# A joined attention and mixture-of-experts kernel: routing groups of 6, 6, 4, 4, 2 and 2 tiles, a narrower running state, and the weight splits of the attention loop partly moved to its ending

## The chip, the core and the metric

The kernel runs on one core of a Trainium2 chip. The metric is the device time of one execution in microseconds (us); the median of three runs is given. Engines are named as in the profile: PE (TensorE) multiplies matrices, PEld is its weight loading, DVE is VectorE, ACT is ScalarE, POOL is GpSimd, SP is the engine whose queue starts most transfers.

## The reference

Three layers, one after the other, all in float32:

```
state = alpha[t] * state + k[t] (outer) v[t];  y[t] = q[t] @ state      # 4 batches x 8 heads, 768 steps, head size 48
x = y as [3072 tokens, 384]
idx = argmax(normalised x @ normalised emb.T / tau); gate = softmax(...)[idx]
x2 = gate * (relu(x @ w1[idx]) @ w2[idx])                                # 8 experts, 384 -> 1024 -> 384
out = elu(x2 @ w_in) @ w_out                                            # 384 -> 2048 -> 384
```

## The kernel before, in words

**Tiles.** The 768 steps are cut into 6 chunks of 128, the work into 24 tiles (chunk times batch); tile i belongs to batch i mod 4. Within a tile the recurrence is done as matrix products: the decays are accumulated by two scans on DVE, R (backwards, line 311) and A (forwards, line 321); POOL makes the scaled keys Kh (line 314) and queries Qh (line 323) from them; PE forms the scores psS (line 351), DVE masks them into P (line 358, two halves), PE multiplies P with the values (line 374) and the queries with the running state G (line 371) into psY, and makes the tile's contribution psU to the state (line 382). DVE adds psU to G (line 394), and ACT scales G by the chunk's decay (line 406). There are four states G, one a batch, each with its own 128-wide slices per pair of heads of which 112 columns are used; the two off-diagonal blocks of a pair are computed and are zero or unused by construction of the value tile `vt`, 176 wide per pair (`VW`).

**Rows and routing.** PE turns psY into token rows and logits in one product (psX, line 419, step `stD`); ACT copies the rows out to `xt`, takes their squares, and DVE reduces the logits `lg` (line 424). When a group of tiles (`GROUPS`: 8, 8, 4, 2 and 2 tiles) is done, DVE finds each token's expert (`stR1`), PE counts places (`stR2`), DVE makes the row numbers `pos_i`, then come the gates (`stX`, `gates`). Each tile's rows are then scaled on ACT (`scale_x`) and scattered to the experts' regions in DRAM by an indirect transfer from POOL (`put`, line 529, after a small memset `tick`).

**The loop.** All of this is written out by hand in program order. In turn i (i = 0 to 21 of `fast`) SP loads tile i+3, PE does the scores of tile i+1, DVE the scans of tile i+2 and P of tile i+1, PE the output of tile i. Every engine works through its own list in this order. `todo` holds the small routing operations on DVE, of which a turn does at most 12. In turn i > 9 one piece of the first expert's weights is split into a rounded part `whi` (ACT, line 175) and a rest `wlo` (DVE, line 178): 12 pieces in all, each rest done in the turn after its `whi` (list `lag`), and each rest starting the load of another piece (`load_w`). `ending` does the last two tiles, the last routing groups, and the first expert's rows: those of the last two tiles come by a product with a one-hot matrix (`hot`, `first_x`, line 541), the rest by a load of the scattered rows (`xr`, line 249) which waits for all earlier scatters, and they meet in the same accumulators (line 893).

**After the loop.** Eight experts, then the dense layer: PE is busy there nearly all the time. None of that is edited.

Of the kernel before, what the change touches and what calls it, by code (L numbers as in the profile page):

```python
# [25 lines left out]
C2 = 112  # L26
TP = T + 1
SW = H // 2 * TP + 1
VW = 176
# [5 lines left out]
GROUPS = [list(range(8)), list(range(8, 16)), list(range(16, 20)), [20, 21], [22, 23]]  # L35
NMID = 9
AHEAD = 4
NG = len(GROUPS)
# [21 lines left out]
def fused_kernel(ctx, tc, qk, a, v, emb, w12, wi, wo, cst, sel, cols, out):  # L60
# [91 lines left out]

    def load_w(n=1):

        for _ in range(n):
            if nload[0] < len(pieces):
                e, s, j = pieces[nload[0]]
                t = stage.tile([128, PW], F32, tag="raw", name="raw")
                nc.sync.dma_start(out=t, in_=w12[e, :, s * SLOT + j * PW:s * SLOT + (j + 1) * PW])
                raw[nload[0]] = t  # L160
                nload[0] += 1

    def split_piece(lag=None):

        if npc[0] >= len(pieces):
            return
        n = npc[0]
        e, s, j = pieces[n]
        npc[0] += 1
        if j == 0:  # L170
            whi[e, s] = ring.tile([128, SLOT], F32R, tag="whi", name="whi")
            wlo[e, s] = ring.tile([128, SLOT], F32R, tag="wlo", name="wlo")
        sl = slice(j * PW, (j + 1) * PW)
        h, l, r = whi[e, s], wlo[e, s], raw.pop(n)
        nc.scalar.activation(out=h[:, sl], in_=r, func=AF.Copy)  # L175

        def low_part():
            nc.vector.tensor_tensor(l[:, sl], r, h[:, sl].bitcast(F32), op=ALU.subtract)  # L178
            load_w()

        if lag is None:
            low_part()
        else:
            lag.append(low_part)
# [76 lines left out]
    def attention():  # L261
        with ExitStack() as st:
# [5 lines left out]
            sm = st.enter_context(tc.tile_pool(name="sm", bufs=2))  # L268
            psD = st.enter_context(tc.tile_pool(name="psD", bufs=2, space=PS))
# [4 lines left out]
            G = [gp.tile([C2, NP, 128], F32, name=f"G{b}") for b in range(B)]  # L274
# [87 lines left out]
            def stC(i):  # L362
# [6 lines left out]
                if cc:  # L369
                    for p in range(NP):  # L370
                        nc.tensor.matmul(y[:, p], G[b][:, p], qh[:, p], start=(p == 0), stop=False)
                for p in range(NP):
                    for h2 in range(2):
                        nc.tensor.matmul(y[HP * h2:HP * (h2 + 1), p], vv[:, p, C2 * h2:C2 * h2 + HP], pp[:, h2, p], start=(cc == 0 and p == 0), stop=(p == NP - 1))
# [12 lines left out]
            def stG(i):  # L387

                if i not in U_:
                    return  # L390
                g3 = G[i % B][:, :, :C2]
                u3 = U_.pop(i)[:, :, :C2]
                if i >= B:
                    nc.vector.tensor_tensor(g3, u3, g3, op=ALU.add)
                else:
                    nc.vector.tensor_copy(g3, u3)

            def stH(i):

                if i >= NT:  # L400
                    return
                r = Rs.pop(i)
                if i >= B:
                    g = G[i % B]
                    for p in range(NP):
                        nc.scalar.activation(out=g[:, p, :C2], in_=g[:, p, :C2], func=AF.Copy, scale=seg(r)[:, p, 1:2])
# [140 lines left out]
            def general():  # L547
# [15 lines left out]
                with tc.For_i(0, NC, 1) as cc, tc.For_i(0, T // TB, 1) as tb:  # L563
                    ts = bass.ds(tb * TB, TB)
                    for b in range(B):
                        for p in range(NP):
                            for h2 in range(2):
                                p0 = (b * H + 2 * p + h2) * EG
                                ch = slice(h2 * HP, h2 * HP + D)
                                for nm, src in (("a", a[bass.ds(cc, 1), ch, b, bass.ds(tb * TB + (p * TP + 1), TB)]),  # L570
# [5 lines left out]
                                    in_=v[bass.ds(cc, 1), ts, b, p, C2 * h2:C2 * h2 + D].rearrange("o t (g e) -> (o g) t e", g=EG))  # L576
# [32 lines left out]
            def fast():  # L609
# [44 lines left out]
                for i in range(tail):  # L654
# [46 lines left out]
                    for j in putq[:2 if len(putq) > 5 else 1]:  # L701
# [6 lines left out]
                    if 9 <= i < 9 + AHEAD * PIECES:  # L708
                        split_piece(lag)
# [30 lines left out]
            def ending():  # L740
# [14 lines left out]
                x3 = stX(g2 - 1)  # L755
                run(x3 + gates(g2 - 1), late)
# [42 lines left out]
                pk[-1]()  # L799
                return xr, t0  # L800
# [366 lines left out]
def _layout(inputs):  # L1167
# [21 lines left out]
    for h2 in range(2):  # L1189
        vv[..., C2 * h2:C2 * h2 + D] = v6[..., h2, :]  # L1190
# [44 lines left out]
```

## Time and profile before

| | |
|---|---|
| median of 3 runs | 849.19 us (848.91 to 854.18) |
| profiled execution, time / span | 844.74 us / 843.0 us |
| PE, PEld, DVE, ACT, POOL busy in the span | 94%, 85%, 64%, 43%, 23% |
| granted clock of PE, mean | 0.984 of full speed |
| attention (loop and ending) | from 0 to about 182 us |
| experts and dense layer | about 182 to 843 us |

The busy shares of the whole span are those of the experts and the dense layer, which are four fifths of the time. The edits lie in the first fifth, so the profile has to be read by stage there: the busy times of a stretch, the engines' instructions in order of time, and what each waited for. A row of the timeline gives start, duration, engine, line, operation, output and inputs with their shapes, a count of merged instructions, and in brackets the idle time before it and what ended that. One float32 matmul of the program shows as two records.

### The profile page before, as it was taken

The numbers are of one execution on the slowest core, as the hardware profiler recorded it, in microseconds if no ns is written. First come the engines' busy times: TensorE is split into PE (matmuls) and PEld (weight loads), VectorE is DVE, ScalarE is ACT, GpSimd is POOL, SyncE is SP. The second block draws the span as 40 slices with busy tenths as digits, with TensorE's granted clock in tenths as the row PEclk, the third lists the DMA queues.
The fourth block names the chain that finished last, engine by engine and source line by source line (L and its number), as shares of the span: only waits on it lengthen the run. The fifth ranks groups of instructions, "written<-read, shape, count | busy, mean of one in ns | idle before, by whom it ended". The sixth has DMA issues, their size and how long they took to land.

```text
span 843.0 us, 13005 instructions
## 1 busy us (share of the span) xinstructions
PE 794.8 (94%) x4876; PEld 716.9 (85%) x4876; DVE 541.5 (64%) x997; ACT 361.6 (43%) x761; POOL 196.8 (23%) x218
## 2 busy tenths in 40 slices
PE   7797987789999999999999999999999999999996
PEld 5687876659988888999989889999999999999995
DVE  7787999846867757777556675545545545555442
ACT  2454775824544434554344543333333333333331
POOL 6333475722323324334200002002002002001102
PEclk9798999999999998999999999999999999999999
DMA  9599687545676774866200001001001000000001
GB/s 259 142 261 250 202 258 212 169 136 160 177 175 190 169 158 144 208 154 204 31 1 2 1 1 37 1 1 38 1 1 37 1 1 29 10 1 10 29 1 37
DMA packets 45234, 82.19 MB, mean 98 GB/s; under 512 B 11624, under 2 KB 18024, under 8 KB 45168
## 3 DMA queue, kind: packets, MB, share of 16 engines
q1 hardware_dynamic: 38512, 71.86, 32.0%
q0 software_dynamic: 3072, 9.45, 3.1%
q8 instruction: 39, 0.64, 0.3%
q10 hardware_dynamic: 3584, 0.01, 0.3%
q14 instruction: 27, 0.22, 0.1%
HBM read 69.10 MB, written 12.22 MB: 96 GB/s over the span
## 4 chain that ended last, share of the span: by engine, by line
PE 67%; DVE 4%; DMA 3%; ACT 2%; issue 1%; POOLq 0%; POOL 0%; SPq 0%; ACTq 0%; DVEq 0%
PE h L1092 21%; PE o L1115 7%; PE o L1113 7%; PE o L1114 7%; PE y L939 4%; PE y L940 4%; PE y L941 4%; PE h L910 4%; PE h L911 4%; PE h L909 4%; PE t L891 1%; DMA raw<-in_wo_dram 1%; DVE dlo L234 1%; DMA raw<-in_wi_dram 1%; DVE g L1098 1%; DVE mn L1094 1%
## 5 line engine op out<-in xcount | busy, mean ns | idle before, releaser
L1094 DVE TENSOR_SCALAR mn<-h 128x512 f32<-128x512 f32 x96 | 66.2, 689 | 139.1 <-PE h L1092 139.1
L1095 ACT ACTIVATE mn<-mn 128x512 f32<-128x512 f32 x96 | 60.7, 632 | 171.9 <-DVE mn L1094 171.9
L1115 PE MATMUL o<-dwo,gl 128*128 128x384 f32 x384 | 129.4, 337 | 1.4 <-DVE gl L1102 1.4
L1114 PE MATMUL o<-dlo,gh 128*128 128x384 f32 x384 | 128.4, 334 | 0.0
L1113 PE MATMUL o<-dwo,gh 128*128 128x384 f32 x384 | 128.2, 334 | 0.0
L1092 PE MATMUL h<-xh,dwi 128*128 128x512 f32 x288 | 112.7, 391 | 0.6 <-ACT x2T L953 0.6
L1092 PE MATMUL h<-xh,dlo 128*128 128x512 f32 x288 | 113.2, 393 | 0.0
L1092 PE MATMUL h<-xl,dwi 128*128 128x512 f32 x288 | 112.5, 392 | 0.0
L1124 POOL DMA_INDIRECT out_dram<-ob,ids x24 | 23.5, 981 | 369.7 <-DVE ob L1119 171.1
L1101 ACT ACTIVATE gh<-g 128x512 fp32r<-128x512 f32 x96 | 60.7, 633 | 77.6 <-DVE g L1098 77.6
L178 DVE TENSOR_TENSOR wlo<-raw,whi 128x512 fp32r<-128x512 f32 x96 | 77.6, 832 | 5.9 <-ACT whi L175 5.9
L913 ACT ACTIVATE hh<-h 128x432 fp32r<-128x432 f32 x64 | 33.9, 530 | 106.7 <-PE h L911 99.6
L1098 DVE SCALAR_TENSOR_TENSOR g<-mn,h 128x512 f32<-128x512 f32 x96 | 66.1, 688 | 16.0 <-ACT mn L1095 15.9
L1113 PEld LDWEIGHTS o<-dwo,gh 128*128 128x128 f32 x384 | 72.0, 187 | 4.2
L1114 PEld LDWEIGHTS o<-dlo,gh 128*128 128x128 f32 x384 | 72.0, 187 | 4.0
L939 PE MATMUL y<-hh,whi 128*128 128x432 f32 x192 | 71.9, 375 | 2.5 <-ACT hh L913 2.5
L1115 PEld LDWEIGHTS o<-dwo,gl 128*128 128x128 f32 x384 | 72.2, 188 | 2.1 <-DVE gl L1102 1.7
L914 DVE SCALAR_TENSOR_TENSOR hl<-h,hh 128x432 fp32r<-128x432 f32 x64 | 38.7, 604 | 54.8 <-ACT hh L913 53.5
L218 POOL TENSOR_SCALAR dg<-dg 128x384 f32<-128x384 f32 x32 | 41.4, 1292 | 131.1 <-ACT dg L217 131.1
L940 PE MATMUL y<-hl,whi 128*128 128x432 f32 x192 | 69.7, 363 | 2.1 <-DVE hl L914 2.1
L909 PE MATMUL h<-xh,whi 128*128 128x432 f32 x192 | 69.8, 364 | 0.7 <-ACTq L966 0.7
L911 PE MATMUL h<-xh,wlo 128*128 128x432 f32 x192 | 69.5, 362 | 0.0
(193 smaller groups left out, 1539.1 us busy)
## 6 DMA issues: line engine op xcount, KB each, us to landing
raw<-in_w_dram SPq DMA_DIRECT2D x96, 256.0 KB, 3.2
qk<-in_qk_dram SPq DMA_DIRECT2D x24, 448.0 KB, 6.2
vt<-in_v_dram SPq DMA_DIRECT2D x24, 352.0 KB, 6.9
raw<-in_wi_dram SPq DMA_DIRECT2D x16, 384.0 KB, 4.4
raw<-in_wo_dram SPq DMA_DIRECT2D x16, 384.0 KB, 4.5
at<-in_alpha_dram SPq DMA_DIRECT2D x24, 226.2 KB, 4.8
xr<-xs SPq DMA_DIRECT2D x7, 576.0 KB, 7.2
xs<-zero SPq DMA_DIRECT2D x7, 288.8 KB, 8.4
```

The lines of the kernel that those rows point to most:

```text
L178: nc.vector.tensor_tensor(l[:, sl], r, h[:, sl].bitcast(F32), op=ALU.subtract)
L909: nc.tensor.matmul(ps, wh, xh[:, kk], start=(kk == 0), stop=False)
L911: nc.tensor.matmul(ps, wl, xh[:, kk], start=False, stop=(kk == KD - 1))
L939: nc.tensor.matmul(acc[e][d], wh, hh, start=(f == 0), stop=False)
L940: nc.tensor.matmul(acc[e][d], wh, hl, start=False, stop=False)
L1092: nc.tensor.matmul(ps, l, x, start=(n == 0), stop=(n == len(terms) - 1))
L1094: nc.vector.tensor_scalar(mn, ps, 0.0, None, op0=ALU.min)
L1095: nc.scalar.activation(out=mn, in_=mn, func=AF.Exp)
L1098: nc.vector.scalar_tensor_tensor(g, mn, -1.0, ps, op0=ALU.add, op1=ALU.max)
L1113: nc.tensor.matmul(o_, gh[:, sl], wh, start=(f == 0), stop=False)
L1114: nc.tensor.matmul(o_, gh[:, sl], wl, start=False, stop=False)
L1115: nc.tensor.matmul(o_, gl[:, sl], wh, start=False, stop=(f == M - 1))
```

## The change

1. The value tile is 128 wide per pair of heads in place of 176 (`VW`), and the state's off-diagonal blocks are no longer computed: psU is 48 wide, G 64 wide, the product of queries and state is done per head (8 products of 48 rows and 64 columns in place of 4 of 112 rows and 128 columns).
2. The addition of psU to G moves from DVE to PE (a product of G with the identity opens psU's accumulation), and ACT copies the sum back into G, at the head of the next turn.
3. `GROUPS` is 6, 6, 4, 4, 2, 2.
4. The first four weight pieces are split as before; the rests (`wlo`) of the other eight are put off to `ending` (`split_spare`: two, one and five of them). Their raw pieces stay in a pool of their own (`early`, 8 buffers). `load_w` is called once a turn from turn 5 on, no longer from the rest.
5. In a turn `put` comes after `stA` and the second half of P, so that POOL does Qh ahead of the scatter; the second `put` of a turn and the second `scale_x` are allowed with one tile less waiting.
6. In `ending`, `stD` of tile 22 comes ahead of `stR2` of the fifth group.

```diff
-VW = 176
+VW = 128
-GROUPS = [list(range(8)), list(range(8, 16)), list(range(16, 20)), [20, 21], [22, 23]]
+GROUPS = [list(range(6)), list(range(6, 12)), list(range(12, 16)), list(range(16, 20)), [20, 21], [22, 23]]
+DIRECT = 4
+    def split_spare(n):
+        for _ in range(n):
+            if spare:
+                spare.pop(0)()
     def load_w(n=1):
...
-                t = stage.tile([128, PW], F32, tag="raw", name="raw")
+                pool = early_p[0] if DIRECT <= nload[0] < AHEAD * PIECES else stage
+                t = pool.tile([128, PW], F32, tag="raw", name="raw")
...
         def low_part():
             nc.vector.tensor_tensor(l[:, sl], r, h[:, sl].bitcast(F32), op=ALU.subtract)
-            load_w()
...
-            G = [gp.tile([C2, NP, 128], F32, name=f"G{b}") for b in range(B)]
+            G = [gp.tile([C2, NP, HP], F32, name=f"G{b}") for b in range(B)]
...
                 if cc:
                     for p in range(NP):
-                        nc.tensor.matmul(y[:, p], G[b][:, p], qh[:, p], start=(p == 0), stop=False)
+                        for h2 in range(2):
+                            rows = slice(HP * h2, HP * h2 + D)
+                            nc.tensor.matmul(y[HP * h2:HP * (h2 + 1), p], G[b][rows, p], qh[rows, p], start=(p == 0), stop=False)
...
-                    u = psG.tile([C2, NP, 128], F32, tag="g", name="psU")
+                    u = psG.tile([C2, NP, D], F32, tag="g", name="psU")
                     kk = Kt.pop(i)
+                    if cc:
+                        nc.tensor.matmul(u, c["ident"][:C2, :C2], G[b][:, :, :D], start=True, stop=False)
                     for p in range(NP):
                         for h2, (m0, m1) in enumerate(((0, HP), (HP, C2))):
-                            nc.tensor.matmul(u[m0:m1, p, :C2], kk[:, p, m0:m1], vv[:, p, D * h2:D * h2 + C2], start=True, stop=True)
+                            nc.tensor.matmul(u[m0:m1, p], kk[:, p, m0:m1], vv[:, p, HP * h2:HP * h2 + D], start=(cc == 0 and p == 0), stop=(p == NP - 1))
...
             def stG(i):
-                g3 = G[i % B][:, :, :C2]
-                u3 = U_.pop(i)[:, :, :C2]
-                if i >= B:
-                    nc.vector.tensor_tensor(g3, u3, g3, op=ALU.add)
-                else:
-                    nc.vector.tensor_copy(g3, u3)
+                if i in U_:
+                    nc.scalar.activation(out=G[i % B][:, :, :D], in_=U_.pop(i), func=AF.Copy)
...
-                    if 5 <= i < 5 + 2 * PIECES:
+                    if 5 <= i:
                         load_w()
+                    stG(i - 1)
...
                     stR(i + 2)
-                    stG(i - 1)
                     stP(i + 1, 0)
+                    stA(i + 2)
+                    stP(i + 1, 1)
                     if putq and place[putq[0]][0] in gated:
                         put(putq.pop(0))
-                    stA(i + 2)
-                    stP(i + 1, 1)
-                    if len(putq) > 4 and place[putq[0]][0] in gated:
+                    if len(putq) > 3 and place[putq[0]][0] in gated:
                         put(putq.pop(0))
...
                     if 9 <= i < 9 + AHEAD * PIECES:
-                        split_piece(lag)
+                        split_piece(lag if i < 9 + DIRECT else spare)
...
                 x3 = stX(g2 - 1)
+                load_w()
+                split_spare(2)
                 run(x3 + gates(g2 - 1), late)
...
+                stD(i, True)
                 r = stR2(g2)
-                stD(i, True)
                 x2 = stX(g2)
                 run(r, x2 + gates(g2))
+                split_spare(1)
...
                 dec[-1]()
                 pk[-1]()
+                split_spare(5)
                 return xr, t0
```

**Where instructions move.** PE, the output and state of one tile in the loop, before (`psY` is the output, `psU` the contribution to the state, `vt` the values, `Kt` the turned keys):

```order
L419 MATMUL psX<-rhsX,yT 128x104 x4
L371 MATMUL psY<-Qh,G_127 128x128 x4
L374 MATMUL psY<-P,vt_123 64x128 x8
L382 MATMUL psU<-vt_123,Kt 64x112
L382 MATMUL psU<-vt_123,Kt 48x112
```

and changed, the same place:

```order
L428 MATMUL psX<-rhsX,yT 128x104 x4
L384 MATMUL psY<-Qh,G_128 64x128 x8
L387 MATMUL psY<-P,vt_124 64x128 x8
L394 MATMUL psU<-G_128,cs 112x192
L397 MATMUL psU<-vt_124,Kt 64x48
L397 MATMUL psU<-vt_124,Kt 48x48
```

The last two rows repeat four times in both. One product with G has become two half-size ones, a product with the identity (`cs`) of 192 columns is new, and psU's products have 48 columns in place of 112.

DVE, one turn of the loop, before (a turn that begins with the rest of a weight piece, and then the routing's first operations):

```order
L178 TENSOR_TENSOR wlo<-raw,whi 128x512
L311 SCALAR_TENSOR_TENSOR R<-at,back 112x517
L312 RECIPROCAL fore_130<-R 112x4
L394 TENSOR_TENSOR G_124<-psU,G_124 112x4x112
L358 TENSOR_TENSOR P<-psS,cs 128x512
L321 SCALAR_TENSOR_TENSOR A<-at,fore_130 112x517
L358 TENSOR_TENSOR P<-psS,cs 128x512
L424 TENSOR_REDUCE lg<-psX 128x8
L463 TENSOR_REDUCE mx<-lg 128x8
```

and changed, the turn ahead of the third group's routing:

```order
L322 SCALAR_TENSOR_TENSOR R<-at,back 112x517
L323 RECIPROCAL fore_133<-R 112x4
L369 TENSOR_TENSOR P<-psS,cs 128x512
L332 SCALAR_TENSOR_TENSOR A<-at,fore_133 112x517
L369 TENSOR_TENSOR P<-psS,cs 128x512
L433 TENSOR_REDUCE lg<-psX 128x8
L472 TENSOR_REDUCE mx<-lg 128x4
```

The addition to G is gone from every turn, the rest `wlo` from all turns but four.

POOL, three turns in the middle of the loop, before (`DMA xs` is the scatter):

```order
L314 TENSOR_TENSOR Kh<-qk,R 112x512
L528 MEMSET tick 1x1
L529 DMA xs<-xt,pos_i 25600x385
L323 TENSOR_TENSOR Qh<-qk,A 112x512
L314 TENSOR_TENSOR Kh<-qk,R 112x512
```

and changed:

```order
L325 TENSOR_TENSOR Kh<-qk,R 112x512
L334 TENSOR_TENSOR Qh<-qk,A 112x512
L537 MEMSET tick 1x1
L538 DMA xs<-xt,pos_i 25600x385
L325 TENSOR_TENSOR Kh<-qk,R 112x512
```

The scatter has gone from between Kh and Qh to behind Qh.

## Rows read from the trace of the kernel before

**Rows 1.** Windows: stretch, length, busy time of each engine, PEclk, DMA share, GB/s
```profile
42.00:73.00 31.00, 27.87 (x363) 25.57 (x361) 22.96 (x34) 17.90 (x52) 10.64 (x9) 1.00 0.99 264
73.00:155.00 82.00, 67.93 (x838) 61.76 (x836) 80.46 (x158) 54.52 (x157) 44.43 (x42) 0.96 0.78 219
```

**Rows 2.** Timeline of DVE: turns 7 and 9, whose scans wait for a transfer
```profile
58.84 1.23 DVE L311 TENSOR_TENSOR_SCAN R<-at,back 112x517 f32<-112x517 f32 x1 [2.13 <-DMA at<-in_alpha_dram]
...
72.84 1.23 DVE L311 TENSOR_TENSOR_SCAN R<-at,back 112x517 f32<-112x517 f32 x1 [2.51 <-DMA at<-in_alpha_dram]
```

**Rows 3.** The page's transfers: KB each, median us from issue to landing
```profile
vt<-in_v_dram SPq DMA_DIRECT2D x24, 352.0 KB, 6.9
```

**Rows 4.** Timeline of DVE: turn 16, two routing turns, the loop's last scan
```profile
117.75 1.22 DVE L311 TENSOR_TENSOR_SCAN R<-at,back 112x517 f32<-112x517 f32 x1
...
119.10 0.59 DVE L394 TENSOR_TENSOR G<-psU,G 112x448 f32<-112x448 f32 x1
...
120.21 1.23 DVE L321 TENSOR_TENSOR_SCAN A<-at,fore 112x517 f32<-112x517 f32 x1
...
122.03 1.99 DVE L178 TENSOR_TENSOR wlo<-raw,whi 128x512 fp32r<-128x512 f32 x1
123.95 1.22 DVE L311 TENSOR_TENSOR_SCAN R<-at,back 112x517 f32<-112x517 f32 x1
...
128.60 1.16 DVE L464 TENSOR_TENSOR e__1640<-lg,mx 128x64 f32<-128x64 f32 x1
...
131.71 1.23 DVE L311 TENSOR_TENSOR_SCAN R<-at,back 112x517 f32<-112x517 f32 x1
...
136.50 0.97 DVE L508 TENSOR_SCALAR pos_i<-pos 128x8 int32<-128x8 f32 x1
...
139.53 1.23 DVE L311 TENSOR_TENSOR_SCAN R<-at,back 112x517 f32<-112x517 f32 x1
...
152.85 1.70 DVE L321 TENSOR_TENSOR_SCAN A<-at,fore 112x517 f32<-112x517 f32 x1
```

**Rows 5.** Timeline of POOL in turn 16
```profile
120.47 1.78 POOL L529 DMA_INDIRECT xs<-xt,pos_i  x1 [0.16 <-ACT xt L432]
122.28 1.18 POOL L323 TENSOR_TENSOR Qh<-qk,A 112x512 f32<-112x512 f32 x1
```

**Rows 6.** Timeline of PE in turn 16 (psT, 4 records at 118.41, left out)
```profile
117.32 1.16 PE L351 MATMUL psS<-Qh,Kh 48*128 48x128 f32 x16 [0.92 <-POOL Qh L323]
...
118.85 1.05 PE L419 MATMUL psX<-rhsX,yT 128*128 128x104 f32 x8
119.74 1.08 PE L371 MATMUL psY<-Qh,G 112*128 112x128 f32 x8
120.75 1.09 PE L374 MATMUL psY<-P,vt 128*64 128x128 f32 x16
121.67 0.94 PE L382 MATMUL psU<-vt,Kt 128*64 128x112 f32 x16
```

**Rows 7.** Groups by line and form: a copy out of PSUM on ACT
```profile
L376 ACT ACTIVATE yT<-psY 128x512 f32<-128x512 f32 x24 | 14.1, 588 | 5.8 <-PE psY L374 5.8
```

**Rows 8.** Timeline of DVE in the ending
```profile
156.93 0.68 DVE L178 TENSOR_TENSOR wlo<-raw,whi 128x512 fp32r<-128x512 f32 x1
...
167.96 0.19 DVE L424 TENSOR_REDUCE lg<-psX 128x8 f32<-128x32 f32 x1 [1.09 <-ACT sq L435]
...
179.82 0.61 DVE L931 TENSOR_TENSOR xl<-t,xh 128x432 fp32r<-128x432 f32 x1 [3.38 <-ACT xh L930]
```

**Rows 9.** Timeline of POOL in the ending, first and last of thirteen scatters
```profile
156.78 1.01 POOL L529 DMA_INDIRECT xs<-xt,pos_i  x1 [0.18 <-issue]
...
172.05 0.96 POOL L529 DMA_INDIRECT xs<-xt,pos_i  x1 [0.23 <-issue]
```

**Rows 10.** Timeline of PE in the ending
```profile
172.79 3.17 PE L541 MATMUL t<-hot,xt 128*128 128x432 f32 x8 [1.05 <-ACT xt L519]
...
177.94 1.28 PE L893 MATMUL t<-cs,xr 128*128 128x128 f32 x8 [0.21 <-DMA xr<-xs]
```

More of the change, by code (lines that the diff above doesn't have):

```diff
@@ L151, in fused_kernel @@
     npc = [0]
+    early_p, spare = [], []
+    def split_spare(n):
+        for _ in range(n):
+            if spare:
+                spare.pop(0)()
     def load_w(n=1):
@@ L268, in attention @@
             sm = st.enter_context(tc.tile_pool(name="sm", bufs=2))
+            early_p.append(st.enter_context(tc.tile_pool(name="early", bufs=AHEAD * PIECES - DIRECT)))
             psD = st.enter_context(tc.tile_pool(name="psD", bufs=2, space=PS))
@@ L370, in stC @@
                     for p in range(NP):
-                        nc.tensor.matmul(y[:, p], G[b][:, p], qh[:, p], start=(p == 0), stop=False)
+                        for h2 in range(2):
+                            rows = slice(HP * h2, HP * h2 + D)
+                            nc.tensor.matmul(y[HP * h2:HP * (h2 + 1), p], G[b][rows, p], qh[rows, p], start=(p == 0), stop=False)
                 for p in range(NP):
                     for h2 in range(2):
-                        nc.tensor.matmul(y[HP * h2:HP * (h2 + 1), p], vv[:, p, C2 * h2:C2 * h2 + HP], pp[:, h2, p], start=(cc == 0 and p == 0), stop=(p == NP - 1))
+                        nc.tensor.matmul(y[HP * h2:HP * (h2 + 1), p], vv[:, p, HP * h2:HP * (h2 + 1)], pp[:, h2, p], start=(cc == 0 and p == 0), stop=(p == NP - 1))
                 yT[i] = wk.tile([128, NP, T], F32, name="yT")
@@ L387, in stG @@
             def stG(i):
-                if i not in U_:
-                    return
-                g3 = G[i % B][:, :, :C2]
-                u3 = U_.pop(i)[:, :, :C2]
-                if i >= B:
-                    nc.vector.tensor_tensor(g3, u3, g3, op=ALU.add)
-                else:
-                    nc.vector.tensor_copy(g3, u3)
+                if i in U_:
+                    nc.scalar.activation(out=G[i % B][:, :, :D], in_=U_.pop(i), func=AF.Copy)
             def stH(i):
@@ L405, in stH @@
                     for p in range(NP):
-                        nc.scalar.activation(out=g[:, p, :C2], in_=g[:, p, :C2], func=AF.Copy, scale=seg(r)[:, p, 1:2])
+                        nc.scalar.activation(out=g[:, p, :D], in_=g[:, p, :D], func=AF.Copy, scale=seg(r)[:, p, 1:2])
             xt, lg = {}, {}
@@ L575, in general @@
                                     out=rv[p0:p0 + EG],
-                                    in_=v[bass.ds(cc, 1), ts, b, p, C2 * h2:C2 * h2 + D].rearrange("o t (g e) -> (o g) t e", g=EG))
+                                    in_=v[bass.ds(cc, 1), ts, b, p, HP * h2:HP * h2 + D].rearrange("o t (g e) -> (o g) t e", g=EG))
                     for t in range(TB):
@@ L700, in fast @@
                     stH(i + 2)
-                    for j in putq[:2 if len(putq) > 5 else 1]:
+                    for j in putq[:2 if len(putq) > 4 else 1]:
                         if place[j][0] in gated and j not in scaled:
@@ L755, in ending @@
                 x3 = stX(g2 - 1)
+                load_w()
+                split_spare(2)
                 run(x3 + gates(g2 - 1), late)
@@ L1189, in _layout @@
     for h2 in range(2):
-        vv[..., C2 * h2:C2 * h2 + D] = v6[..., h2, :]
+        vv[..., HP * h2:HP * h2 + D] = v6[..., h2, :]
     r = {"qk": qk, "alpha": al, "v": vv}
```

## The prediction, made before the changed kernel was run

> **What bounds the kernel now.** I read the busy times by stretch first, then the timelines of DVE, POOL and PE in one turn, then the waits at both ends. From 182 us on nothing is edited, and PE is full there; only the first 182 us can change. Between 42 and 73 us the transfers bound: DMA share 0.99 at 264 GB/s [rows 1], and the R scans of turns 7 and 9 wait 2.13 and 2.51 us for their decays [rows 2]. From 73 to 155 us DVE bounds: busy 80.46 of 82 us, while PE has 67.93, ACT 54.52, POOL 44.43 [rows 1]. In turn 16 (one R scan to the next, 117.75 to 123.95, 6.20 us) DVE has no gap, and PE waits 0.92 us for Qh [rows 4, 6]. From 155 to 182 us three chains run side by side: DVE's routing, which ends in `first_x` at 172.79, thirteen scatters on POOL to 173.0 and the row load behind them, which lands 0.21 us after `first_x` is done [rows 9, 10].
>
> **Value tiles.** 352 becomes 256 KB [rows 3], 96 KB less a tile. Before the R scan of turn 9 four such loads (tiles 7 to 10) lie in the transfer-bound stretch: 0.39 MB at 264 GB/s [rows 1] is 1.5 us. So that scan starts at 71.3 in place of 72.84 [rows 2]. The routing of the first group now falls into turns 7 and 8; at 6.55 us a routing turn (below) the two take 13.1 us, and the transfers give them 14.0 now (58.84 to 72.84 [rows 2]), 13.2 later: covered, just.
>
> **DVE's turn.** What leaves is the addition to G, 0.51 us to the next start, and in eight turns a rest `wlo`: 0.68 us alone [rows 8], 1.99 in turn 16 [rows 4]. The long one ends 0.56 us after POOL's Qh, which runs from 122.28 to 123.46 [rows 4, 5]: that subtraction does not get on while POOL multiplies. The small ones at 128.60 (1.16 us) and 136.50 (0.97) are lengthened too [rows 4]. Qh could have started at the end of A, 121.44, but for the scatter ahead of it: 0.84 us late [rows 4, 5]. With the scatter behind Qh those operations end up to 0.84 earlier; I take 0.6, with ends 0 and 0.84. The 0.5 for G I do not book: without it A starts sooner after R and runs into Kh, and the A scans of the stretch run from 1.23 to 1.70 us [rows 4]. So R to the end of A stays at 3.6 to 3.7 us, and a turn without routing needs 4.4 us on DVE, 5.45 with one of the four `wlo` left (3.6 + 1.25 of Qh + 0.6).
>
> A routing turn was 7.76 and 7.82 us (123.95 to 131.71 to 139.53 [rows 4]); less `wlo` (0.6) and 0.6 of waiting for Qh it is 6.55. The count of small operations hardly depends on the group's size, so the sixth group is a real addition, but it falls into the transfer-bound turns.
>
> **PE's turn.** Scores to the end of psU is 117.32 to 122.61, 5.3 us [rows 6]. Added: the identity product, two records of 192 columns; a record takes 0.11 us at 104 columns [rows 6] and 0.40 at 432 [rows 10], so 0.19 each, 0.37 us (ends 0.22 and 0.79). psU's 16 records go from 112 to 48 columns: between unchanged and 0.94 scaled to 0.40 [rows 6]; I take 0.2 saved, less than half of that, as no 64-wide records of the trace follow each other faster than these. The product with G becomes 16 half-size records in place of 8: the neighbours of 16 take 0.92 (psY) and 1.09 (psS to psT), the old one 1.01, so nothing either way, 0.1 as bound [rows 6]. Three more changes of product shape: the one from G's product to psY costs at most 0.12 (1.01 us where the eight records before it took 0.89 [rows 6]), so 0 to 0.36. Sum 5.5 us, ends 4.9 and 6.5. The Trainium skill, page "TensorEngine Tiling (Array Packing)", section "Key Properties", speaks against the edit: it has the array drained whenever the tile shape changes; by it the three changes cost their full 0.36, the turn is nearer 5.9, the six turns that PE bounds lose 0.4 each, turn 10 0.15, and the time is 842.2 in place of 839.7. The page "TensorE: Matmul & The Clock Gate", section "LDWEIGHTS (loading the stationary operand)", lets a weight load take time by its columns alone; by it psU would save nothing, as its weights keep 64 columns. No run here shows either apart yet.
>
> **ACT, POOL and SP.** ACT takes over a copy of at most 0.59 us [rows 7] a turn and scales 48 columns in place of 112; it is idle for 27 of 82 us [rows 1], about 2 a turn: nothing. POOL does the same work in another order; Kh waits behind a scatter of up to 1.78 us [rows 5], but the scores that need it are a turn away: nothing. `load_w` starts the same 18 pieces, one a turn, without waiting for a `wlo`: nothing, or a little. Over 13 turns of 5.6 us a turn loads 930 KB, a piece of 256 and about one scatter of 197: 1.4 MB, 250 GB/s, under the 264 seen [rows 1].
>
> **Sum of the loop.** From the R scan of turn 9 to the end of the last A it was 72.84 to 154.55, 81.7 us [rows 2, 4]. Now: turns 9, 11, 12, 15, 16 at PE's 5.5 (27.5); 10, with gates and a `wlo`, 5.75; 13, routing with the last `wlo`, 7.15; 14, 17 and 18, routing, 6.55 (19.65); 19, without psT, 5.1; 20, with gates, 5.2; R to the end of A in 21, 3.6. Together 73.95: 7.75 less. With the 1.5 above, 9.25.
>
> **The ending.** DVE gets three `wlo` in the routing chain, 0.6 each, and loses one; the 0.84 of the delayed Qh comes back through tile 23's scores, and DVE's wait of 1.09 for the last squares [rows 8] takes up the third `wlo`: about 0. The `wlo` at 156.93 ran at 0.68 beside a scatter at 156.78 [rows 8, 9], so I price them so. The five after the row counts need 3.0 us and find DVE idle for 3.38 [rows 8]; without that gap they would delay `xl` by up to 3.0. Scatters between the last Qh and the row load: thirteen at 1.27 us (156.78 to 172.05 [rows 9]) become ten, but the last four still wait for gates and row numbers from DVE; 0.25 us gained, since `first_x` is the other half of that meeting. `stD` ahead of `stR2` only lets tile 22's product start before a wait that tile 23's must pass anyway. Bounds: 1.5 either way.
>
> The profiled execution (844.74, span 843.0) loses 9.25 + 0.25 = 9.5, so 835.2; the median of the runs lies 4.45 above it, and I forecast **839.7 us**.
>
> **Rivals.**
> - *PE takes DVE's place.* Turns cost 6.5 on PE (serial half-size products, every drain paid): turns 9, 11, 12, 15, 16 and 19 lose 1 us each and turn 10 0.75, so 6.75 of the 9.5 is gone: 846.5. For it: PE is idle only 0.92 of 6.20 us in turn 16, and the change adds PE work. Against: the 16 records of psY take 0.92 us, the 8 full-size ones of G's product 1.01 [rows 6]: half-size records run at half the price. The drains that the tiling page has belong to this case.
> - *More comes free.* PE at 4.9 with psU scaled to its 48 columns (turns 9, 15, 16 and 19 0.6 each, 11 and 12 0.05: 2.5 us) and the shorter chain of scatters worth 1.1: 836.1. For it: PE's own list has no other wait in turn 16. Against: `first_x` does not move with the scatters.
> - *Slower: the eight rests come back on the ending's chain.* If each takes 1.99 us there as in turn 16, they cost 15.9; less the one removed (0.6) and DVE's idle 1.09 and 3.38 [rows 8] the ending is 10.85 longer, which outweighs the loop's 9.25: 850.8. It turns the sign from 1.8 us a rest. Against: no POOL multiplication runs after the last Qh, and the one seen beside a scatter took 0.68.
>
> **How the numbers follow.** Forecast 0.60, with its own range 836 to 844 (0.6 us more or less on each of the four routing turns; ending 1.5); PE 0.20; more free 0.13; rests 0.04; something unnamed 0.03. Range 834 to 847. Faster by over 1% (8.5 us, about what a measurement of this kernel can tell from no change) means under 840.7: all of "more free" and two thirds of the forecast, 0.53; slower by over 1% needs two things to go wrong, 0.04; the rest, 0.43, is within.
>
> **What would show it.** In the changed profile: no additions to G on DVE, and the stretch from the R scan of turn 9 to the last A near 74 us with DVE at about 0.85 to 0.9 busy; PE from scores to the end of psU near 5.5 us and back to back in plain turns; Qh directly after A; routing turns near 6.5; `wlo` near 0.68 in the ending. Wrong would be PE's turn at 6 or more, routing turns still above 7, a wait for the decays beyond turn 9 (transfers bound on), or `xl` waiting for the five rests.

## The result, and the profile after

The changed kernel takes 838.79 us (median of 4 runs, 838.62 to 841.67), where before took 850.04 on the same chip: a ratio of 0.9875 with a 95% interval of [0.9847, 0.9904]. On another chip, where before took 844.37, the unedited change took 838.89: 0.9941 [0.9919, 0.9963]. It is faster on both, by 0.6 to 1.25%; the time of the change is the same on the two chips, and that of before is not. One run among the experiments (848.87 us, at a granted clock of 0.962 where its kernel's other runs had 0.978 to 0.982) was in a slower state and is left out everywhere below.

The profiled execution takes 838.67 us (span 836.9), 6.07 less than that of before. Its rows, beside those shown ahead. First the windows [rows 1], columns as there:

```profile
42.00:73.00 31.00, 30.22 (x414) 25.75 (x414) 25.66 (x53) 17.97 (x57) 10.63 (x9) 1.00 1.01 258
73.00:155.00 82.00, 74.13 (x992) 62.88 (x992) 73.28 (x157) 58.88 (x186) 49.50 (x53) 0.96 0.78 217
```

DVE was busy 80.46 of 82 us and is now 73.28: neither DVE nor PE (74.13) is full, so something else is waited for. DVE's timeline [rows 2, 4, 8]:

```profile
57.77 1.23 DVE L322 TENSOR_TENSOR_SCAN R<-at,back 112x517 f32<-112x517 f32 x1 [1.83 <-DMA at<-in_alpha_dram]
...
71.92 1.24 DVE L322 TENSOR_TENSOR_SCAN R<-at,back 112x517 f32<-112x517 f32 x1
...
99.52 0.69 DVE L369 TENSOR_TENSOR P<-psS,cs 128x512 f32<-128x512 f32 x1 [5.06 <-PE psS L362]
...
142.86 2.43 DVE L332 TENSOR_TENSOR_SCAN A<-at,fore 112x517 f32<-112x517 f32 x1
...
148.69 1.22 DVE L332 TENSOR_TENSOR_SCAN A<-at,fore 112x517 f32<-112x517 f32 x1
...
150.85 2.25 DVE L473 TENSOR_TENSOR e__2114<-lg,mx 128x32 f32<-128x32 f32 x1
...
164.43 0.67 DVE L188 TENSOR_TENSOR wlo<-raw,whi 128x512 fp32r<-128x512 f32 x1
...
174.45 3.08 DVE L188 TENSOR_TENSOR wlo<-raw,whi 128x512 fp32r<-128x512 f32 x5
177.46 0.59 DVE L944 TENSOR_TENSOR xl<-t,xh 128x432 fp32r<-128x432 f32 x1
```

The R scan of turn 9 no longer waits (71.92 against 72.84). The last A scan ends at 149.91 against 154.55. In between DVE stands still for 5.06 us and waits for scores (psS). PE at the same place, one plain turn and then the gap [rows 6]:

```profile
82.97 1.16 PE L362 MATMUL psS<-Qh,Kh 48*128 48x128 f32 x16
84.06 0.60 PE L346 MATMUL psT<-cs,Kh 112*128 112x112 f32 x4
84.50 1.05 PE L428 MATMUL psX<-rhsX,yT 128*128 128x104 f32 x8
85.48 1.09 PE L384 MATMUL psY<-Qh,G 48*64 48x128 f32 x16
86.50 1.09 PE L387 MATMUL psY<-P,vt 128*64 128x128 f32 x16
87.52 0.58 PE L394 MATMUL psU<-G,cs 112*112 112x192 f32 x2
88.03 0.67 PE L397 MATMUL psU<-vt,Kt 128*64 128x48 f32 x16
88.63 1.16 PE L362 MATMUL psS<-Qh,Kh 48*128 48x128 f32 x16
...
97.40 2.08 PE L362 MATMUL psS<-Qh,Kh 48*128 48x128 f32 x16 [3.05 <-POOL tick L537]
```

From scores to scores it is 5.66 us, back to back. Then PE is idle for 3.05 us, and the next sixteen records take 2.08 in place of 1.16: the granted clock fell after the gap (mean 0.90 from 80 to 100 us, and 0.50, the lower of its two levels, 1.2 GHz, from 98 to 102). What PE waited for stands on POOL [rows 5, 9]:

```profile
87.02 1.18 POOL L334 TENSOR_TENSOR Qh<-qk,A 112x512 f32<-112x512 f32 x1 [1.24 <-DMA vt<-in_v_dram]
92.03 1.14 POOL L538 DMA_INDIRECT xs<-xt,pos_i  x1 [3.84 <-DMA at<-in_alpha_dram]
...
93.48 1.54 POOL L538 DMA_INDIRECT xs<-xt,pos_i  x1 [0.20 <-issue]
95.04 1.19 POOL L325 TENSOR_TENSOR Kh<-qk,R 112x512 f32<-112x512 f32 x1
96.18 1.17 POOL L334 TENSOR_TENSOR Qh<-qk,A 112x512 f32<-112x512 f32 x1
...
146.79 2.01 POOL L538 DMA_INDIRECT xs<-xt,pos_i  x1
...
149.11 1.58 POOL L538 DMA_INDIRECT xs<-xt,pos_i  x1 [0.21 <-issue]
150.70 1.20 POOL L325 TENSOR_TENSOR Kh<-qk,R 112x512 f32<-112x512 f32 x1
151.84 1.20 POOL L334 TENSOR_TENSOR Qh<-qk,A 112x512 f32<-112x512 f32 x1
```

The first scatter waits 3.84 us, and Kh and Qh of tile 14, whose scans were done at 89.9 and 91.8, stand behind it and its follower. Such a pair of scatters stands ahead of Kh of tile 23 in turn 20 too, and a small DVE operation (0.44 us in another run, below) lasts 2.25 beside Kh and Qh. The ending [rows 10]:

```profile
170.65 3.39 PE L550 MATMUL t<-hot,xt 128*128 128x432 f32 x8
...
175.64 3.61 PE L906 MATMUL t<-cs,xr 128*128 128x128 f32 x24
179.18 0.47 PE L922 MATMUL h<-xh,whi 128*128 128x432 f32 x1
```

The loaded rows are no longer waited for, and PE goes from their products straight to the first expert product. That one starts at 179.18; in the trace of before it is

```profile
181.82 0.47 PE L909 MATMUL h<-xh,whi 128*128 128x432 f32 x1
```

So the edited stage gives 2.64 of the 6.07 us; 3.43 come from the part behind it, which nobody edited.

### The profile page after: what moved, and what is told of

It is laid out like the page before. It is cut to its first block, busy times and chain, and to the rows that moved or that the text cites. A ratio compares the mean times of both kernels' runs of the same rounds, so it can differ in the third digit from the quotient of the medians.

```text
span 836.9 us, 13417 instructions
## 1 busy us (share of the span) xinstructions
PE 799.5 (96%) x5070; PEld 713.7 (85%) x5070; DVE 538.8 (64%) x1006; ACT 360.9 (43%) x782; POOL 195.3 (23%) x218
## 4 chain that ended last, share of the span: by engine, by line
PE 63%; DMA 6%; DVE 5%; ACT 2%; issue 1%; ACTq 0%; POOLq 0%; POOL 0%; SPq 0%; DVEq 0%
PE h L1105 21%; PE o L1128 7%; PE o L1126 7%; PE o L1127 7%; PE y L952 4%; PE y L953 3%; DMA raw<-in_wi_dram 3%; PE y L954 3%; PE h L923 3%; PE h L924 3%; PE h L922 3%; DMA raw<-in_wo_dram 1%; PE t L904 1%; DVE dlo L244 1%; DMA xr<-xs 1%
## 5 line engine op out<-in xcount | busy, mean ns | idle before, releaser
L188 DVE TENSOR_TENSOR wlo<-raw,whi 128x512 fp32r<-128x512 f32 x96 | 73.8, 796 | 5.8 <-ACT whi L185 4.9
L923 PE MATMUL h<-xl,whi 128*128 128x432 f32 x192 | 69.3, 361 | 0.2 <-DVEq L979 0.2
```

The source lines that it names most:

```text
L923: nc.tensor.matmul(ps, wh, xl[:, kk], start=False, stop=False)
```

## The experiments

Twelve kernels, in three sets of four, each set on one chip beside before (843.71, 844.37 and 846.62 us). Only the second set holds a run of the change (838.89); in the other two, times are set beside the 838.79 and 838.89 of the change on other chips. The columns are: ratio to before with its 95% interval; and from the profile, in us, the start of the R scan of turn 9, from there to that of turn 21, from there to the first expert product, and what is left of the span.

| run | ratio | R of 9 | 9 to 21 | ending | rest |
|---|---|---|---|---|---|
| before, as shown ahead | | 72.84 | 78.08 | 30.90 | 661.2 |
| before again | | 72.12 | 79.42 | 30.63 | 656.8 |
| change | 0.9875 [0.9847, 0.9904] | 71.92 | 74.84 | 32.42 | 657.7 |
| change again | 0.9941 [0.9919, 0.9963] | 71.25 | 76.50 | 31.23 | 656.4 |
| narrow state alone | 0.9971 [0.9957, 0.9984] | 70.24 | 79.14 | 36.08 | 655.1 |
| change, rests in loop | 0.9998 [0.9974, 1.0022] | 72.06 | 78.91 | 30.63 | 657.3 |
| change, put ahead of Qh | 1.0026 [0.9993, 1.0058] | 70.59 | 83.77 | 32.15 | 657.0 |
| change, scatters held | 0.99 [0.9866, 0.9934] | 70.18 | 72.10 | 31.56 | 656.9 |
| held, one scatter at the end | 0.9902 [0.987, 0.9934] | 71.26 | 71.80 | 31.02 | 657.3 |
| change, POOL memsets | 0.9882 [0.9841, 0.9923] | 72.45 | 71.09 | 30.86 | 659.2 |
| change, old groups | 0.99 [0.9862, 0.9938] | 70.66 | 72.14 | 32.18 | 658.5 |
| memsets, G on DVE | 0.9845 [0.9823, 0.9866] | 71.78 | 71.62 | 32.63 | 657.4 |
| memsets, one scatter at the end | 0.9852 [0.9835, 0.9868] | 70.53 | 71.09 | 34.80 | 656.1 |
| memsets, put ahead of Qh | 0.9872 [0.9846, 0.9898] | not read | | | |

**Before again.** No edit.

> The kernel before, unedited, for a second profile: the profiled run of before (844.74 us) was some 5 us under the median of its runs, while that of the change was a usual one. If the slack lies in the part after attention, this run shows the first expert matmul again near 181.8 us and over 661.2 us behind it (up to 666). If attention itself varies, the first expert matmul comes at up to 186 us and 661 us follow; then the edited stage gains more than the 2.64 us that the first pair of profiles gives it.

840.82 us. The first expert product is at 182.17, and 656.8 follow. So the part behind attention varies by itself: over the thirteen traces it is 655.1 to 661.2, with no relation to an edit that these traces show, and the first profile of before holds the longest. Both expectations missed: that profile was not quick there but slow.

**The first scatter of a turn between Kh and Qh again.**

```diff
+                    if putq and place[putq[0]][0] in gated:
+                        put(putq.pop(0))
                     stA(i + 2)
                     stP(i + 1, 1)
-                    if putq and place[putq[0]][0] in gated:
-                        put(putq.pop(0))
```

> The change with one part undone: the first scatter of a turn stands between Kh and Qh again, as before. Theory A (the place costs as I priced it, Qh late by up to 0.84 us in each turn with a scatter, about ten turns, part of it hidden where PE bounds): 2 to 5 us slower than the change, 841 to 844 us, most of it spread over the turns. Theory B (the place is worth nothing, as Kh behind the scatters now pays what Qh paid): within 1 us of the change, 838 to 840. Theory C (the first scatter's wait for the zero fills decides): it then holds up Qh of tile 13 in place of Kh of tile 14, a turn sooner, and one turn loses about 5.8 us where the change loses 3.05: 841.5, all of the difference before 100 us.

845.89 us, and 7.3 to 8.9 us longer from turn 9 to turn 21 than the two profiles of the change: more than any theory had. The scatter starts at 91.86 here, though Kh ahead of it was done at 84.16: it waits 7.69 us, and until the same time as in the change. That pointed at something outside the scatter's place. But only 4.8 us of the loss lie in turns 9 to 13. Turn 17 alone takes 9.37 us, where the two profiles of the change have 6.24 and 6.23, and this trace puts that down to the place: Qh of turn 15 stands behind a scatter until 119.88, PE waits for it, and then runs at the lower level of its clock (the second row is the window from 124 to 128 us, columns as above):

```profile
121.12 1.16 PE L362 MATMUL psS<-Qh,Kh 48*128 48x128 f32 x16 [1.59 <-POOL Qh L334]
```

```profile
124.00:128.00 4.00, 4.00 (x33) 3.49 (x34) 3.50 (x8) 1.21 (x4) 1.66 (x2) 0.50 0.37 116
```

**All rests in the loop.** One line: `split_piece(lag if i < 9 + DIRECT else spare)` becomes `split_piece(lag)`.

> The change with one part undone: all twelve rests are done in the loop, none in the ending. Theory A (PE's turn of 5.66 us bounds the plain turns, DVE the routing turns): the four or five routing turns lose 0.7 to 1.3 us each, plain turns (4.4 + 1.25 on DVE, against 5.66) nothing, the ending gives back 0.6 to 1.3: 2 to 5 us slower than the change, 841 to 844. Theory B (the rests on DVE are the whole gain): eight times 0.98 to 1.25, 8 to 10 us slower, 847 to 849. Theory C (the gain is in transfers and the rests are nothing): within 1 us of the change.

842.85 us; turns 9 to 21 take 78.91, and 2.4 to 4.1 more than the two profiles of the change, while the ending is 0.6 to 1.8 shorter. This is theory A. With a ratio of 0.9998 the rest of the change without this part is worth nothing measurable, as long as the wait on POOL stays.

**Scatters held.** Both conditions of the loop's `put` get `i > 12 and`.

> The change with one edit: no scatter before turn 13, so that none waits for the zero fills ahead of Kh of tile 14. Theory A (that wait is the 3.05 us that PE idles in turn 12, plus its slow clock after it): turn 12 to 13 takes 11.3 us in place of 15.9, and since two scatters fall into more of the later turns some of it is lost again: 1.5 to 4 us faster than the change, 834.5 to 837. Theory B (the transfers bound there anyway, share 1.02 from 80 to 100 us, so the same time is waited for decays or weights a turn later): within 1 us, 838 to 839.5. Theory C (the held scatters come out in the ending): the row load waits for them and the time is 1 to 3 us longer.

833.76 us. Turns 9 to 21 take 72.10, 2.7 less than in the change, and the first expert product is at 173.84 in place of 179.18. This is theory A in direction, and more than it had; theory B falls, as the transfers are as dense (share 1.00 from 73 to 100 us). But the reason in it, the zero fills, falls too: the last of them had landed by 69.64, when, in the change, the load that waits for its semaphore was issued.

**The change again.** No edit.

> The changed kernel, unedited, on the same chip as the three runs beside it: it gives them their base, as the times of before differed between the two sets of runs taken so far (850.04 and 843.71 us). If the ratio of 0.9875 belongs to the kernel and not to a chip, it comes out at 0.985 to 0.990 here, and the profile shows the first scatter waiting to about 92 us again and the first expert matmul near 179 us. If the quick profile of before and the 3.46 us after attention were what made the first ratio, it comes out at 0.992 to 0.995.

838.89 us, ratio 0.9941 [0.9919, 0.9963]: the second expectation. The scatter waits 3.84 us again, to 91.68.

**Held, and no second scatter in turns 20 and 21.** As above, and `if 12 < i < 20 and len(putq) > 3 ...` for the second `put`.

> The change with no scatter before turn 13 (as in the run before) and, besides, no second scatter in turns 20 and 21, so that Kh and Qh of tile 23 come straight after their scans. Theory A (the two scatters ahead of Kh of tile 23 and the 2.24 us in which DVE's small operation ran beside Kh and Qh are the 1.2 us by which the ending starts late): the way from the last A scan to the first expert matmul falls from 28.4 to 26.5 to 27.5 us, 1 to 2 us faster than with the scatters only held, 4 to 6.5 us faster than the change. Theory B (the two scatters that move into the ending hold up the row load there): the same as with the scatters only held, or up to 1.5 us slower; then the first product with loaded rows starts later than 0.2 us after the product before it.

834.31 us, ratio as with the scatters only held; the ending is 0.54 us shorter in the profile. This is theory A at about half of its least gain; the total shows none.

**Memsets on POOL.**

```diff
                     stR(i + 2)
+                    if 2 <= i < 9:
+                        for _ in range(3):
+                            nc.gpsimd.memset(tick, 0.0)
```

> The change with 21 small POOL memsets added in turns 2 to 8, where POOL is idle for two thirds of the time; the first scatter stays in turn 11. It asks what the first scatter waited for from 88.20 to 92.03. The fills had landed by 69.64, as a load that waits for their semaphore was issued then. Theory A (POOL waits for its own instructions: a transfer on the instruction queue ran at 89.0 in the change, 89.0 and 92.0 in the two runs where the scatter then started at 91.86 and 94.58): the memsets move that transfer to an earlier place in the program, the scatter starts at 88.3 to 89, PE's gap of 3.05 us closes, 2.5 to 4.5 us faster than the change. Theory B (it waits for data that land at 92, whatever POOL does): the scatter starts at 91.5 to 92.5 again and the time is within 1 us of the change.

834.34 us against 838.89 for the change in the same set: work was added and the kernel is 4.55 us faster, theory A at the top of its range. POOL after the edit:

```profile
86.89 1.18 POOL L334 TENSOR_TENSOR Qh<-qk,A 112x512 f32<-112x512 f32 x1 [1.24 <-DVE A L332]
88.25 1.40 POOL L538 DMA_INDIRECT xs<-xt,pos_i  x1 [0.17 <-DMA raw<-in_w_dram]
...
89.95 0.96 POOL L538 DMA_INDIRECT xs<-xt,pos_i  x1 [0.21 <-ACT xt L529]
90.93 1.19 POOL L325 TENSOR_TENSOR Kh<-qk,R 112x512 f32<-112x512 f32 x1
```

The transfers by queue (packets, MB, share of the 16 engines) in half a microsecond of the change, 89.0 to 89.5 us:

```profile
q1 hardware_dynamic: 41, 0.09, 80.5%
q14 instruction: 1, 0.01, 7.6%
```

and of the kernel with memsets, 66.5 to 67.0 us:

```profile
q1 hardware_dynamic: 73, 0.13, 85.5%
q14 instruction: 2, 0.02, 12.8%
```

The instruction transfer of 89.0 has gone to 66.5 (beside the one that the change has at 66.0), and none is left on that queue between 67 and 102 us. In the four traces with the wait it ran at 89.0, 88.5, 89.0 and 92.0, and the scatter began at 92.03, 91.68, 91.86 and 94.58: 2.6 to 3.2 us after it each time (the transfers are placed to half a microsecond), wherever the scatter stood. With the scatters held, and with the old groups (below), the transfer ran at 91.0 and 93.5; the first scatter came 6.7 and 7.9 us behind it and waited 0.17. So it did with memsets in two more kernels below, at 88.10 and 86.31. The trace does not say whose instructions a transfer carries; but the memsets, which POOL alone executes, moved it. With them it comes four turns earlier, in a turn in which POOL is busy for half of the time. So POOL waited for its own instructions: this follows from the memsets' effect, and no row says it directly. Why they came late there is not shown; the transfers were full (share 1.02 from 80 to 100 us). The Trainium skill, page "Runtime: NRT & Kernel Launch", section "Instruction fetch mechanics", has an engine's sequencer fetch the next block of instructions through a DMA queue of its own while it executes the current one, at a mostly hidden cost; here 3.84 us of it were not hidden.

**The old groups.** `GROUPS` of 8, 8, 4, 2 and 2 again.

> The change with one part undone: routing groups of 8, 8, 4, 2 and 2 tiles again. Theory A (the groups are worth little by themselves: the first scatter comes two turns later and meets no wait, which gains about the 4 us that holding the scatters gains; one routing group less on DVE, in turns that transfers bound; three more scatters in the ending, about 3.8 us of POOL, of which the row load sees 0 to 2): 2 to 5 us faster than the change. Theory B (the sixth group is what makes the ending short): the row load waits as it did before, the ending is 1.5 to 3 us longer than with the scatters held, and the time is within 1.5 us of the change.

835.15 us. The first scatter comes at 101.35 and waits 0.17; the loaded rows are waited for again (0.50 and 0.47 us), and loop and ending are each about 1 us longer than with the memsets. This is theory A: without POOL's wait the six groups give 2.4 us in these two stretches, but R of turn 9 comes 1.8 later in the trace with memsets (72.45 against 70.66), so that 0.6 is left at the first expert product, and the medians differ by 0.8, less than the runs with memsets do among themselves (832.0 to 835.42). What six groups are worth without the wait is not shown. In the change they lose 3.7 (838.89 against 835.15) by bringing the first scatter to the place where POOL's instructions come late.

**The narrow state alone.** Before, with the first two points of the change and nothing else.

> The kernel before with one part of the change alone: value tiles 128 wide, the running state's products of 48 columns, the addition to G on PE and its copy on ACT. Groups, rests, scatters and weight loads as before. Theory A (DVE bounds a plain turn at 6.2 us and loses the 0.5 us of G's addition, PE's turn of 5.66 stays just under it; value tiles give 1.5): 4 to 7 us faster than before, about half of the change's gain in the loop, plain turns at 5.6 to 5.9 us, routing turns at 7.2 to 7.5. Theory B (PE's longer turn or A scans that run into Kh eat what DVE saves): within 2 us of before, plain turns at 6.0 to 6.3. Theory C (the narrow state is nearly all of the gain): 8 us or more.

843.38 us, 0.9971 [0.9957, 0.9984]: 3.2 us under before, between theory B's 2 and theory A's 4. Plain turns stay at 6.1 to 6.3, as theory B has it, and turns 9 to 21 take 79.14 against 78.08 and 79.42: nothing. What it gains is ahead of turn 9, whose R scan starts at 70.24. The ending of this profile is long, as PE stands still between records of psY (the first three of seven such gaps are shown):

```profile
159.45 0.38 PE L386 MATMUL psY<-P,vt 128*64 128x128 f32 x2 [0.31 <-issue]
...
160.89 0.41 PE L383 MATMUL psY<-Qh,G 48*64 48x128 f32 x2 [0.47 <-issue]
162.31 0.46 PE L383 MATMUL psY<-Qh,G 48*64 48x128 f32 x1 [1.00 <-issue]
```

PE waits there for nothing that the trace shows. The first profile of the change and that of G on DVE have a shorter stretch of this kind (1.1 us of gaps each) and the next longest undisturbed endings, 32.42 and 32.63; the other traces have none in psY. Its cause stays open.

**G added on DVE again, with the memsets.** The product with the identity goes, the addition stands behind the R scan again, and:

```diff
-                    nc.scalar.activation(out=G[i % B][:, :, :D], in_=U_.pop(i), func=AF.Copy)
+                    g3, u3 = G[i % B][:, :, :D], U_.pop(i)
+                    if i >= B:
+                        nc.vector.tensor_tensor(g3, u3, g3, op=ALU.add)
+                    else:
+                        nc.vector.tensor_copy(g3, u3)
```

> The change with the 21 POOL memsets, and one more part undone: G is added on DVE again (192 columns, after the R scan) in place of the product with the identity and the copy on ACT; the state stays narrow. Theory A (plain turns are bound by PE, whose two identity records take 0.51 us; routing turns by DVE, where the addition takes 0.3): plain turns fall from 5.66 to 5.1 to 5.3 us, seven of them, routing turns grow by 0.2 to 0.5, five of them: 0 to 3 us faster than with the memsets alone. Theory B (DVE bounds everywhere, the product is free on PE): every turn grows by 0.3 or more, 3 to 6 us slower. Theory C (G arrives too late on DVE for ACT's scaling and PE's next product): 6 us or more slower, with PE waiting for G.

833.98 us, beside 834.12 for the next kernel of the set. Theories B and C fall. Theory A's total, 0 to 3 us faster than with the memsets alone (834.34, in another set), is just met, but not by its mechanism: no turn got shorter. DVE in turn 16, first with the memsets alone, then with G on DVE:

```profile
113.46 1.22 DVE L322 TENSOR_TENSOR_SCAN R<-at,back 112x517 f32<-112x517 f32 x1
...
115.39 2.43 DVE L332 TENSOR_TENSOR_SCAN A<-at,fore 112x517 f32<-112x517 f32 x1
...
119.31 1.21 DVE L322 TENSOR_TENSOR_SCAN R<-at,back 112x517 f32<-112x517 f32 x1
```

```profile
113.31 1.22 DVE L322 TENSOR_TENSOR_SCAN R<-at,back 112x517 f32<-112x517 f32 x1
...
114.66 0.33 DVE L405 TENSOR_TENSOR G<-psU,G 112x192 f32<-112x192 f32 x1
...
115.50 2.16 DVE L332 TENSOR_TENSOR_SCAN A<-at,fore 112x517 f32<-112x517 f32 x1
...
119.15 1.21 DVE L322 TENSOR_TENSOR_SCAN R<-at,back 112x517 f32<-112x517 f32 x1
```

The turn is 5.85 and 5.84 us. What DVE saves ahead of A, A loses again beside Kh. PE loses 8.33 us of work in the window from 73 to 155 us (75.81 to 67.48) and waits instead (1.53 and 0.59 us for Qh in turns 15 and 16). So with PE's turn at 5.66 DVE's chain is about as long, and moving the addition from PE to DVE changes nothing.

**Memsets, and no second scatter in turns 20 and 21.**

> The change with the 21 POOL memsets and no second scatter in turns 20 and 21. Theory A (both gains add up): 0.3 to 1.3 us faster than with the memsets alone, the small DVE operation beside Kh and Qh of tile 23 back from 2.25 us to under 1.3. Theory B (ACT's scaled rows, not the scatters, set the product with the one-hot matrix): the same within 0.5 us.

834.12 us, 0.9852 [0.9835, 0.9868]. The small operation is back at 0.44 us:

```profile
146.92 0.44 DVE L473 TENSOR_TENSOR e__2133<-lg,mx 128x32 f32<-128x32 f32 x1
```

The ending of this profile ran at a granted clock of 0.66 from 140 to 160 us, so its length says nothing. That it beats the memsets alone is not shown, as they ran in different sets.

**Memsets, and the first scatter between Kh and Qh.**

> The change with the 21 POOL memsets and the first scatter of a turn between Kh and Qh again. It repeats the first experiment without POOL's wait for its instructions, which had held up Qh there by 7.7 us. Theory A (as priced: Qh up to 0.84 us late in DVE's turns, nothing in plain turns): 1.5 to 4 us slower than with the memsets alone. Theory B (most of the 8.9 us that the first experiment lost from turn 9 to turn 21 belongs to the place itself): 5 to 8 us slower. Theory C (the place is worth nothing once POOL does not wait): within 1 us.

834.44 us (median of four runs, 832.14 to 838.24); the profile is that of the run left out, and is not read. The ratio, 0.9872 [0.9846, 0.9898], overlaps that of the kernel just above: theory B falls; A and C are not told apart.

**What was not undone by itself.** No run puts off the rests in the kernel before and changes nothing else, and none undoes point 6, the earlier second `scale_x` or the new place of `load_w` alone. Their shares are not known.

## Why the prediction was right, and where it was not

The time, 839.7, came within 1 us of 838.79, but by a sum that did not hold: 9.5 us were to come from the edited stage, and the profile gives 2.64 there. Two things made up for the missing 6.86 us. The part behind attention, which nobody edited, was 3.43 shorter than in the profile of before. And the forecast added 4.45 us, by which before's median lay above its profile, while the change's median lies 0.12 above its own. That the total came so close is luck; the terms were as follows.

- **Value tiles: right as far as the spread lets one see.** R of turn 9 was to start at 71.3; it starts at 71.92 and 71.25. Over the eleven traces with narrow tiles that were read it is 70.18 to 72.45, in the mean 71.2; the two of before have 72.84 and 72.12. So the booked 1.5 us is less than the traces differ among themselves. In the change the scan waits for decays in turn 7 (1.83) and no longer in turn 9.
- **G off DVE, booked at nothing: right.** The narrow state alone leaves turns 9 to 21 as they were, and G put back on DVE costs nothing: A and Kh collide either way. (The A scans of before ran to 2.03 us in that stretch, at 75.31, and not only to 1.70.)
- **The rests: right in mechanism.** Done in the loop they cost 2.4 to 4.1 us there and give 0.6 to 1.8 back in the ending. In the ending a rest takes 0.67, as priced, and the five delay nothing that PE waits for. Without POOL's wait turns 9 to 21 take 71.09, where the turns of the sum add up to 70.35; but this is in part luck again, as turns 9 and 15 take 4.95 and 4.96 (5.5 in the sum) and turns 12, 18 and 20 take 6.47, 7.24 and 5.82 (5.5, 6.55 and 5.2).
- **PE's turn: a little low.** From scores to the end of psU it is 5.73 where 5.5 was forecast; from scores to scores 5.66, where before has 5.22 (87.42 to 92.64). The identity takes 0.51 (0.37 was taken). psU's records take 0.60 to the next start, a third less than the 0.87 before (0.2 was taken as saved), though their weights keep 64 columns. Another 0.19 went to the ends of psX (0.98, was 0.89) and psY (1.02, was 0.92), where the product's shape now changes. With G on DVE psY leads straight into psU, of the same shape, and takes 0.92 again, so there the change is the cause. The third change lies behind the identity, inside its 0.51, and cannot be read alone; two of three thus cost 0.09 and 0.10, near the 0.12 that each could cost at most. The Trainium skill's page "TensorEngine Tiling (Array Packing)", section "Key Properties", has the array drained at each change of tiling mode; the trace agrees that these changes cost time. That PE bounds plain turns was only half true: DVE's chain is as long.
- **POOL: the step that failed.** It was "the same work in another order ... nothing". The change put two scatters between Qh and the next Kh, and the first of them where POOL waits for instructions. From turn 9 to turn 21 that is 3.75 us in the profiles (74.84 against 71.09; 4.55 in the medians), of which 3.06 lie in turns 12 to 14: the wait, the follower's 1.54, PE's gap, and PE's lower clock behind it. Kh is "a turn away" from its scores only if it starts on time.
- **The ending: not where forecast.** It was to lose 0.25; it is 1.5 and 0.3 longer in the two profiles of the change and even with before (30.86) in the run with the memsets. Part of it is Kh of tile 23 behind two scatters (0.54 between the two kernels with held scatters), and 1.1 us in the first profile are PE's gaps by "issue".
- **What hid the miss.** The 3.43 us behind attention belong to the first profile of before; its second has 656.8 there, the change 657.7 and 656.4. And before's median of 849.19 is that of one chip; on the three other chips before takes 843.7 to 846.6, and the change 838.89 on one of them. What makes before slower on the first chip is open, as no profile of such a run exists.
- **The rivals.** PE in DVE's place did not come (5.66, not 6.5). The rests did not land on the ending's chain. "More comes free" has its time, 836.1, near the kernels without the wait (833.8 to 835.2), though by another way.

## What to carry to other kernels

When an instruction is moved on an in-order queue, price what now stands behind it if it waits, and not only its own duration: a scatter of 1.14 us put ahead of a multiplication of 1.19 cost some 4 us, because it waited 3.84. When a wait ends at the same time in several variants, wherever the waiting instruction stands, look at the instruction transfers too: here the wait belonged to the engine itself. And take two profiles of the base before you book a difference of a few microseconds in a part that nobody edited.

## What the runs showed of the hardware

- An engine that executes few instructions can be held up by its instruction supply: POOL (218 instructions in the span) stood for 3.84 us (7.69 in another order) and went on 2.6 to 3.2 us after a transfer of 8 KB on an instruction queue (28 on that queue carry 0.22 MB), in a stretch where the DMA engines were full. Adding 21 small instructions earlier moved the transfer and removed the wait.
- A DVE operation with both inputs in SBUF, the on-chip memory, makes no progress while POOL multiplies: A takes 2.43 us in place of 1.23 beside a Kh of 1.19, and an operation of 0.44 lasts 2.25 beside Kh and Qh in a row (150.70 to 153.04). P, whose scores come from PSUM, the memory of PE's results, takes 0.66 to 0.69 beside them as without. It goes the other way too: with the memsets, in turn 8, A keeps its 1.23 and Kh takes 2.13.

```profile
67.37 1.23 DVE L332 TENSOR_TENSOR_SCAN A<-at,fore 112x517 f32<-112x517 f32 x1
67.44 2.13 POOL L325 TENSOR_TENSOR Kh<-qk,R 112x512 f32<-112x512 f32 x1 [3.84 <-DMA qk<-in_qk_dram]
```

  The Trainium skill's page "SBUF — State Buffer", section "SBUF: two separate sides", has the two engines' shared ports as a lock that is held for the whole instruction, against a DVE operation with two SBUF inputs; these rows agree.
- PE's granted clock fell to its lower level (0.50) after gaps of 3.05 us (the change) and 1.59 (the scatter ahead of Qh), but not after a gap of 1.53 with G on DVE, where it was 1.00 from 73 to 155 us.
